# Sliding-window attention and a squared-ReLU MLP: three query loads on ScalarE's DMA queue instead of SyncE's

## The chip, the cores and the metric

The kernel runs on one core of a Trainium2 chip. A core has a matrix engine (TensorE, PE in the profile), a vector engine (VectorE, DVE), an activation engine (ScalarE, ACT), a general engine (GpSimd, POOL) and a sequencer that mainly issues transfers (SyncE, SP). Each takes its own instructions in order. They wait for each other by semaphores. Transfers between memory (HBM) and the core's SBUF go through 16 DMA engines. SP, ACT and POOL can each issue a transfer on a queue of their own; the profile calls SP's queue q1, ACT's q10 and POOL's q0.

The metric is the time of one execution on the device, in microseconds (us). Lower is better.

## The reference

Four batches of eight heads, 768 tokens, head dimension 64. Each query sees the first 4 keys (the sinks) and the last 128 keys up to its own. The heads are then joined to a 3072 x 512 matrix, which goes through two matrix products with a squared ReLU between them.

```python
scores = scale * np.matmul(q, k.transpose(0, 1, 3, 2))
keep = is_sink | in_window            # pos < 4, or 0 <= i - j < 128
scores = np.where(keep, scores, -1e9)
a = softmax(scores)
attn = np.matmul(a, v)
x = attn.transpose(0, 2, 1, 3).reshape(3072, 512)
out = np.maximum(x @ w_in, 0.0) ** 2 @ w_out      # 512 -> 2048 -> 512
```

## The kernel before

The batches are worked through one after another. Attention of batch b + 1 is interleaved with the MLP of batch b, so that PE always has something. Heads go in pairs: pair m is heads 2m and 2m + 1, so there are four pairs, 0 to 3. For each pair, keys and queries must stand transposed in SBUF (the tile qkT), with the head dimension on the partitions.

Only batch 0, and of it the first 512 tokens, concerns the change. Its keys and queries come in eight loads of 256 KB, one for each pair and each of keys and queries, all in float32 (`load_qk`, line 305, the issue on line 315). Four tiles `qr` take them: pairs 0 and 2 share a tile for the keys and one for the queries, pairs 1 and 3 two others. Everything else of the inputs (values, weights, the rest of keys and queries) is loaded by POOL's queue, which converts to bfloat16 on the way.

After a load has landed, one engine converts it to bfloat16 and regroups it (`regroup`, line 404, by the helper `copy` on lines 178 to 183; the profile shows qs<-qr). PE transposes the pair's keys and queries into a PSUM bank pt (line 426). ACT and DVE each copy one half of that bank into qkT (`unload`, line 451; qkT<-pt). Then PE can compute scores of the first 256 tokens (line 538, ps<-qkT; with the mask added as a bias on line 531), ACT takes the exponential (line 559), PE multiplies by the values (line 619).

What runs where and in which order is not found at run time. Every piece of work is an operation with a number, and the string `ORDER` (lines 18 to 57) lists numbers with a letter for the engine: `p` PE, `v` DVE, `a` ACT, `g` POOL, `s` SP. `Plan.run` (line 87) issues them in that order, so each engine's instruction stream is the sequence of its letters. `+10` behind a PE operation puts ten filler matmuls ahead of it (`warm`, line 169, profile line L173), which compute nothing that is used; 36 more stand at the start (line 1209). The eight loads are operations 8 to 15, all on SP: keys 0, queries 0, keys 2, queries 2, keys 1, queries 1, keys 3, queries 3. The helper `dma_op` (line 267) makes the operation of a load; its `follow` says that a load must come after the previous one on the same queue.

Who converts what in batch 0, in each engine's order: DVE takes keys 0 and queries 0 (operations 55, 56), then unloads half of pair 0 (59), then queries 2 (66), later queries 3 (71). ACT takes keys 2 (65), then unloads the other half of pair 0 (58), later keys 3 (70). POOL takes keys 1 and queries 1 (60, 61). The first scores on PE (99) need both halves of pair 0.

SP then loads the four sink values of each head for batches 0, 1 and 2 (`vs_in`, line 361); POOL reads those of batch 0 in line 481.

Of the kernel before, what the change touches and what calls it, by code (L numbers as in the profile page):

```python
# [15 lines left out]
ALU = mybir.AluOpType  # L16

ORDER = """
8s 0v 5g 2v 894p+36 1v 6g 55v 9s 4g 3g 56v 57p 10s 65a 11s 12s 59v 58a 99p+10 19g 20g 101a 21g 22g 23g 13s 14s 66v 79p
81a 67p 69v 80p+11 68a 82a 15s 71v 60g 61g 62p+4 63v 100p 7s 70a 72p+9 74v 64a 87p+2 89a 88p 83p 85p 76v 73v 90a 109p  # L20
24g 25g 26g 27g 103a 86v 84v 91p 93p 77p 94v 95p 92v 97p+13 112a 108p 78a 96a 75g 114p+1 98v 105p+1 110a 152p 104g 17s
28g 29g 30g 102v 31g 32g 33g 106p 113v 111v 115p 107v 116v 34g 35g 36g 37g 158p 159a 117p 118a 119p 164p 120v 161p
162a 163a 153a 155p 156v 38g 39g 173p 122p 125p 165v 157v 127v 174a 160a 123v 126v 124a 170p 171v 139p 140p 141a 16s
# [51 lines left out]
class Plan:  # L75
# [5 lines left out]
    def op(self, kind, engines, run, after=(), takes=(), reads=(), dma=None, follow=(), late=()):  # L81
        o = Op(kind, engines.split(), run, after, takes, reads, dma, follow, late)
        o.group, o.idx = self.group, len(self.ops)
        self.ops.append(o)
        return o
# [21 lines left out]
def kernel(  # L107
# [11 lines left out]
    nc = tc.nc  # L119
# [35 lines left out]
    vs_in = consts.tile([32, B, D + 1], FP32)  # L155
# [10 lines left out]
    def tile_of(slot, name, shape, dtype):  # L166
        return pools[slot.pool][slot.buf].tile(shape, dtype, name=name, tag=slot.pool)
# [97 lines left out]
    chained = {}  # L265

    def dma_op(queue, name, run, takes=()):
        o = op("load " + name[0], queue, run, dma=name[0], takes=takes,
               follow=[chained[queue]] if queue in chained and name[0] != "vs_in" else ())
        ops[name] = o  # L270
        if name[0] != "vs_in":
            chained[queue] = o
        o.name = name
        return o
# [3 lines left out]
    def load_w_in(i):  # L278
        c = slice(512 * i, 512 * i + 512)
        w_in_op[i] = dma_op(  # L280
            "pool", ("w_in", i),
            lambda e: nc.gpsimd.dma_start(out=w_in_sb[:, i],
                                          in_=moe_w_in[:, c].rearrange("(a p) f -> p a f", p=128)))

    def load_w_out(i):
        w_out_op[i] = dma_op(
            "pool", ("w_out", i),
            lambda e: nc.gpsimd.dma_start(
                out=w_out_sb[:, 4 * i:4 * i + 4, :],
                in_=moe_w_out[512 * i:512 * i + 512, :].rearrange("(p f) m -> p f m", p=128)))  # L290

    ops, late = {}, {}
    qr_slot, qs_slot = {}, {}
    qn_t, qn_slot, first_tile = {}, {}, {}
    qr_t, qs_t, ex_t, bank_t = {}, {}, {}, {}
# [9 lines left out]
    def load_qk(m, ti):  # L305

        t0, n = GROUPS[0][0]
        share = (m % 2, ti)
        if share not in qr_slot:
            qr_slot[share] = Slot("qr", 2)  # L310

        def run(e):
            if m < 2:
                qr_t[share] = tile_of(qr_slot[share], "qr", [128, 4, n * D], FP32)
            nc.sync.dma_start(out=qr_t[share][:, 2 * (m // 2):2 * (m // 2) + 2, :],
                              in_=(q, k)[ti][0, 2 * m:2 * m + 2, 0:128 * n, :].rearrange("h (p t) d -> p h (t d)", t=n))
        ops["qk", 0, m, ti, 0] = dma_op("sp", ("qk", 0, m, ti, 0), run, [qr_slot[share]] if m < 2 else [])
        qr_slot[0, m, ti, 0] = qr_slot[share]

    def load_tile(b, ti, t, readers=0):  # L320
# [817 lines left out]
    for m in range(2):  # L1138
        for ti in (1, 0):
            load_qk(m, ti)  # L1140
        for ti in (1, 0):
            load_qk(m + 2, ti)
# [104 lines left out]
```

## Time and profile before

| | us |
|---|---|
| median of 3 runs | 210.09 |
| lowest and highest of the 3 | 209.96, 211.04 |
| the profiled execution | 209.37 |
| its span, first to last instruction | 207.7 |

The profile is one execution of the program, recorded by the hardware. Times in its rows are us from the start of the span, unless marked ns. A row of the timeline has the start, the duration, the engine, the line of the code, the operation, what is written and read, and how many instructions were merged; in brackets stands the idle time of the engine ahead of it and what ended it. PEld is PE's loading of weights, SPq and ACTq are the issuing of transfers by SP and ACT. The share of the DMA engines can exceed 1, since one engine can have several packets in hand at once.

### The profile page before, as it was taken

How to read it: one execution, taken by the hardware profiler on the slowest of the kernel's cores; microseconds unless marked ns; L12 is line 12 of the kernel's file. 1: busy time of each engine (PE TensorE's matmuls, PEld its weight loads, DVE VectorE, ACT ScalarE, POOL GpSimd, SP SyncE). 2: the span in 40 equal slices, each digit the busy share in tenths (PEclk: the TensorE clock that was granted, in tenths of full speed). 3: DMA queues.
4: the chain of work that ended last, by engine and by line, in shares of the span. 5: the costliest groups of instructions: out<-in, count | busy, mean ns of one | idle time of the engine just before them, and what ended most of it. 6: DMA issues, size and time to landing. Idle time of an engine off the chain costs nothing.

```text
span 207.7 us, 5646 instructions
## 1 busy us (share of the span) xinstructions
PE 200.7 (97%) x2373; PEld 168.8 (81%) x2373; DVE 164.9 (79%) x303; ACT 129.9 (63%) x169; POOL 93.4 (45%) x136
## 2 busy tenths in 40 slices
PE   7799999999999999999999999999999999999993
PEld 7459997579657966568798889999889999999982
DVE  6377267487998776668989989999997979899953
ACT  2684288747886553698879185499964168694200
POOL 7999275999925998168020019940240000000000
PEclk9999999999999999999999999999999999999999
DMA  5999999999999999999995146995024305000205
GB/s 147 295 185 206 176 197 213 168 171 173 147 145 83 125 108 150 201 158 134 116 203 153 30 152 41 144 195 32 3 51 129 65 14 200 8 0 0 90 14 202
DMA packets 93865, 26.09 MB, mean 126 GB/s; under 512 B 86800, under 2 KB 91536, under 8 KB 93840
## 3 DMA queue, kind: packets, MB, share of 16 engines
q0 software_dynamic: 69248, 12.59, 82.2%
q1 hardware_dynamic: 24032, 12.69, 30.1%
q10 hardware_dynamic: 560, 0.46, 0.7%
q8 instruction: 18, 0.29, 0.6%
q14 instruction: 7, 0.06, 0.1%
HBM read 27.30 MB, written 6.29 MB: 162 GB/s over the span
## 4 chain that ended last, share of the span: by engine, by line
PE 86%; ACT 5%; DVE 4%; DMA 2%; issue 2%; SPq 0%
PE py L1035 27%; PE pm L836 17%; PE pm L696 16%; PE py L925 7%; PE ps L538 5%; PE po L619 5%; ACT expm L559 2%; DMA qr<-in_k_dram 2%; PE pt L436 2%; DVE sg L993 2%; ACT r L707 1%; PE po L594 1%; PE px L664 1%; PE ya L1035 1%; DVE gT_sb L993 1%
## 5 line engine op out<-in xcount | busy, mean ns | idle before, releaser
L559 ACT ACTIVATE expm<-ps 128x1024 bf16<-128x1024 f32 (+1 forms) x48 | 43.6, 952 | 15.3 <-PE ps L538 15.2
L696 PE MATMUL pm<-xT,w_in_sb 128*128 128x256 bf16 (+1 forms) x320 | 44.9, 294 | 0.1
L199 POOL TENSOR_SCALAR_AFFINE_SELECT expm<-expm 128x512 bf16<-128x512 bf16 x30 | 18.4, 644 | 53.3 <-ACT expm L559 53.2
L696 PEld LDWEIGHTS <-w_in_sb 128*128 128x128 bf16 x320 | 34.2, 114 | 6.5 <-issue 1.0
L1035 PEld LDWEIGHTS <-gT_sb 128*128 128x128 bf16 x336 | 30.6, 98 | 4.4 <-issue 0.9
L707 ACT ACTIVATE r<-pm 128x1024 bf16<-128x1024 f32 x17 | 17.3, 1024 | 14.1 <-PE pm L696 14.1
L1035 PEld LDWEIGHTS <-sg 128*128 128x128 bf16 x240 | 22.6, 98 | 2.5
L836 PE MATMUL pm<-xs,w_in_sb 128*128 128x128 bf16 (+1 forms) x256 | 24.2, 246 | 0.1
L836 PEld LDWEIGHTS <-w_in_sb 128*128 128x128 bf16 x256 | 22.4, 114 | 0.3 <-issue 0.2
L341 POOL DMA_DIRECT2D v<-in_v_dram x24 | 22.0, 938 | 0.0
L1035 PE MATMUL py<-wt,gT_sb 128*128 128x256 bf16 x160 | 20.7, 273 | 0.0
L1035 PE MATMUL py<-wt,sg 128*128 128x256 bf16 x160 | 20.7, 273 | 0.0
L858 ACT ACTIVATE gT_sb<-r 128x1024 bf16<-128x1024 bf16 x19 | 19.2, 1056 | 0.9 <-DVE r L904 0.8
L1035 PE MATMUL py<-w_out_sb,gT_sb 128*128 128x256 bf16 x144 | 18.7, 273 | 0.0
L330 POOL DMA_DIRECT2D qn<-in_k_dram x20 | 18.1, 917 | 1.0 <-DMA qn<-in_q_dram 0.7
L330 POOL DMA_DIRECT2D qn<-in_q_dram x20 | 17.9, 919 | 0.4 <-PE po L619 0.3
L635 DVE TENSOR_TENSOR xn_sb<-po,rc 128x512 bf16<-128x512 f32 (+1 forms) x26 | 16.9, 650 | 0.9
L836 PEld LDWEIGHTS <-qkT 128*128 128x128 bf16 x192 | 16.3, 113 | 0.1
L877 DVE TENSOR_TENSOR t<-t,pm 128x512 f32<-128x512 f32 x24 | 15.6, 682 | 0.9 <-PE pm L836 0.7
L538 PE MATMUL ps<-qkT 64*128 64x128 bf16 (+1 forms) x256 | 14.7, 238 | 1.5 <-ACT qkT L180 1.5
L892 ACT ACTIVATE r<-pm 128x1024 bf16<-128x1024 f32 x12 | 11.9, 1023 | 6.4 <-PE pm L836 5.5
L925 PE MATMUL py<-w_out_sb,gT_sb 128*128 128x512 bf16 x64 | 15.3, 380 | 0.0
(96 smaller groups left out, 326.5 us busy)
## 6 DMA issues: line engine op xcount, KB each, us to landing
out_dram<-osb SPq DMA_DIRECT2D x11, 512.0 KB, 3.5
v<-in_v_dram POOLq DMA_DIRECT2D x24, 128.0 KB, 6.1
qn<-in_k_dram POOLq DMA_DIRECT2D x20, 128.0 KB, 7.6
qn<-in_q_dram POOLq DMA_DIRECT2D x20, 128.0 KB, 5.8
w_in_sb<-in_moe_w_in_dram POOLq DMA_DIRECT2D x4, 512.0 KB, 10.1
w_out_sb<-in_moe_w_out_dram POOLq DMA_DIRECT2D x4, 512.0 KB, 10.5
qr<-in_k_dram SPq DMA_DIRECT2D x4, 256.0 KB, 5.6
qr<-in_q_dram SPq DMA_DIRECT2D x4, 256.0 KB, 5.6
```

The source lines that it names most:

```text
L199: nc.gpsimd.affine_select(out=e_tile, in_=e_tile, compare_op=ALU.is_ge, fill=fill, base=i - 1, pattern=[[0, n], [1 if i else -1, 128]], ch ...
L330: nc.gpsimd.dma_start(out=qn_t[b, ti][:, t, :].rearrange("p (h d) -> p h d", d=D), in_=(q, k)[ti][b, :, 128 * t:128 * t + 128, :].rearrang ...
L341: nc.gpsimd.dma_start(out=v_sb[b % 2][:, t, :, 0:D], in_=v[b, :, 128 * t:128 * t + 128, :].rearrange("h p d -> p h d"))
L538: nc.tensor.matmul(ps[:, h2, o:o + w], lhsT=qkT_sb[r, m, 1, c, :], rhs=qkT_sb[r, m, 0, qb:qb + w // 128, :], start=(i == 0 and not biased) ...
L559: nc.scalar.activation(out=x[:, :, o:512], in_=bank_t["s", b, s, m][:, :, o:512], func=AF.Exp, scale=scale)
L635: touch(("po", b, s, m0), e, nc.vector.tensor_tensor(out=xn_sb[:, 2 * s:2 * s + 2, :].rearrange("p i (j q h d) -> q p j i h d", j=2, q=2, ...
L696: nc.tensor.matmul(pm[:, i, :], lhsT=w_in_sb[:, fb // 4, kb, fb % 4:512:4], rhs=xT[:, c0 // 256:(c0 + cw) // 256, kb, :], start=(kb == 0), ...
L707: nc.scalar.activation(out=o, in_=h, func=AF.Relu)
L836: touch(tag, e, nc.tensor.matmul(y[:, bk, i, :], lhsT=weights(name, f0 + i, a), rhs=rhs[:, a, :], start=fresh and i == 0 and a == 0, stop= ...
L858: nc.scalar.activation(out=d, in_=x, func=AF.Square)
L925: touch((b, u), e, nc.tensor.matmul(pm[:, i, :], lhsT=gT_sb[:, fb, 128 * t:128 * t + 128], rhs=w_out_sb[:, fb, :], start=(fb == 0), stop=( ...
L1035: ins = nc.tensor.matmul(y_, lhsT=x[:, i, :], rhs=r_, start=(first or tail and n == 2) and i == 0, stop=i == HB - 1, skip_group_check=not ...
```

## The change

The queries of pairs 2, 1 and 3 (operations 11, 13 and 15) get the letter `a` instead of `s`: ACT issues them, on its own queue. The queries of pair 0 and all keys stay on SP. In `ORDER` the eight loads now stand together near the front; for SP and ACT only the sequence of their own letters counts.

```diff
-8s 0v 5g 2v 894p+36 1v 6g 55v 9s 4g 3g 56v 57p 10s 65a 11s 12s 59v 58a 99p+10 19g 20g 101a 21g 22g 23g 13s 14s 66v 79p
-81a 67p 69v 80p+11 68a 82a 15s 71v 60g 61g 62p+4 63v 100p 7s 70a 72p+9 74v 64a 87p+2 89a 88p 83p 85p 76v 73v 90a 109p
+8s 0v 5g 2v 894p+36 1v 6g 55v 9s 10s 11a 12s 13a 14s 15a 4g 3g 56v 57p 65a 59v 58a 99p+10 19g 20g 101a 21g 22g 23g 66v
+79p 81a 67p 69v 80p+11 68a 82a 71v 60g 61g 62p+4 63v 100p 7s 70a 72p+9 74v 64a 87p+2 89a 88p 83p 85p 76v 73v 90a 109p
...
     def dma_op(queue, name, run, takes=()):
         o = op("load " + name[0], queue, run, dma=name[0], takes=takes,
-               follow=[chained[queue]] if queue in chained and name[0] != "vs_in" else ())
+               follow=[chained[queue]] if queue == "pool" and queue in chained else ())
...
-            nc.sync.dma_start(out=qr_t[share][:, 2 * (m // 2):2 * (m // 2) + 2, :],
-                              in_=(q, k)[ti][0, 2 * m:2 * m + 2, 0:128 * n, :].rearrange("h (p t) d -> p h (t d)", t=n))
-        ops["qk", 0, m, ti, 0] = dma_op("sp", ("qk", 0, m, ti, 0), run, [qr_slot[share]] if m < 2 else [])
+            (nc.scalar if e == "act" else nc.sync).dma_start(
+                out=qr_t[share][:, 2 * (m // 2):2 * (m // 2) + 2, :],
+                in_=(q, k)[ti][0, 2 * m:2 * m + 2, 0:128 * n, :].rearrange("h (p t) d -> p h (t d)", t=n))
+        ops["qk", 0, m, ti, 0] = dma_op("sp act", ("qk", 0, m, ti, 0), run, [qr_slot[share]] if m < 2 else [])
```

The instruction streams show it at two places. First SP, from the start of the kernel, as it was before (qr_190 and qr_254 are the tiles of pairs 0 and 2, qr_282 and qr_310 those of pairs 1 and 3; k and q tell keys from queries):

```order
L315 DMA qr_190<-in_k_dram 128x2x256
L315 DMA qr_254<-in_q_dram 128x2x256
L315 DMA qr_190<-in_k_dram 128x2x256
L315 DMA qr_254<-in_q_dram 128x2x256
L315 DMA qr_282<-in_k_dram 128x2x256
L315 DMA qr_310<-in_q_dram 128x2x256
L315 DMA qr_282<-in_k_dram 128x2x256
L315 DMA qr_310<-in_q_dram 128x2x256
L361 DMA vs_in_178<-in_v_dram 32x1x64 x3
```

The eight loads stand in one queue, keys 2 third, the sink values behind them. The same place on SP after the change (the keys of pairs 1 and 3 have the tile qr_258; lines behind 315 have moved by one):

```order
L315 DMA qr_190<-in_k_dram 128x2x256
L315 DMA qr_254<-in_q_dram 128x2x256
L315 DMA qr_190<-in_k_dram 128x2x256
L315 DMA qr_258<-in_k_dram 128x2x256 x2
L362 DMA vs_in_178<-in_v_dram 32x1x64 x3
L949 DMA out_0_dram<-osb_960 128x1024
```

Keys 0, queries 0 and keys 2 keep their places; keys 1 and 3 and the sink values move up by one, two and three places. Second, ACT from the start of the kernel, before:

```order
L180 ACT_TABLE_LOAD
L180 ACTIVATE qs_279<-qr_190 128x512
L180 ACTIVATE qkT0_179<-pt_261 128x2x256
L559 ACTIVATE expm_305<-ps_286 128x1024
L559 ACTIVATE expm_322<-ps_315 128x2x384
```

Its first work behind the loading of its function table is the regrouping of keys 2, then half the unloading of pair 0. After the change:

```order
L315 DMA qr_254<-in_q_dram 128x2x256
L315 DMA qr_260<-in_q_dram 128x2x256 x2
L180 ACT_TABLE_LOAD
L180 ACTIVATE qs_286<-qr_190 128x512
L180 ACTIVATE qkT0_179<-pt_269 128x2x256
L560 ACTIVATE expm_309<-ps_290 128x1024
```

The queries of pairs 2, 1 and 3, in that order, stand ahead of the table load; the rest of ACT's stream is unchanged. PE, DVE and POOL execute the same instructions in the same order as before.

## The prediction

> **What bounds the kernel now.** I read the page first, for the engine that is busy and the mix of the chain.
>
> ```profile
> span 207.7 us, 5646 instructions
> PE 200.7 (97%) x2373; PEld 168.8 (81%) x2373; DVE 164.9 (79%) x303; ACT 129.9 (63%) x169; POOL 93.4 (45%) x136
> PE 86%; ACT 5%; DVE 4%; DMA 2%; issue 2%; SPq 0%
> ```
>
> TensorE (PE) is busy for 97% of the span, and the chain of work that ended last lies on it for 86%. DMA has 2% of that chain, some 4 us, so the next view is the table of waits, for PE alone over the whole span.
>
> ```profile
> PE ps L538 <- ACT qkT L180: 1.5, 1, 1.5
> PE warm L1209 <- DVE ones L207: 1.1, 1, 1.1
> PE pk L499 <- ACT expm L559: 0.3, 1, 0.3
> ```
>
> After its start, PE waits once for long: 1.5 us, for the unloading of the first transposes by ScalarE (ACT). The longest of its later waits is 0.3 us. So the place to look at is the first 8 us, and anything that makes the first scores later has no slack to fall into. The chain of waits, cut to the first 30 us, tells what stands ahead of that unloading (start, duration, what):
>
> ```profile
> 1.32 0.46 SPq L315
> ...
> 1.82 4.46 DMA qr<-in_k_dram
> ...
> 6.31 0.63 ACT qs L180
> 6.94 0.49 ACT qkT L180
> ...
> 7.47 0.40 PE ps L538 x6
> ```
>
> The load that is issued at 1.82 us, the third on SP's queue, is the keys of pair 2. It lands at 1.82 + 4.46 = 6.28. ACT then regroups them (its first real instruction), unloads half of pair 0's transposes, and PE starts the scores at 7.47. ACT takes its instructions in order, so the unloading of pair 0, whose transposes are done at 5.3 us (below), stands behind the keys of pair 2. **The landing of the third load sets when PE really begins.**
>
> The landings of the later loads stand in the issue lists of three stretches of 0.1 us, each holding the issues that overlap it (last column: us from issue to landing):
>
> ```profile
> qr<-in_q_dram SPq DMA_DIRECT2D x1, 256.0 KB, 5.1
> qr<-in_k_dram SPq DMA_DIRECT2D x1, 256.0 KB, 5.4
> ...
> qr<-in_q_dram SPq DMA_DIRECT2D x1, 256.0 KB, 5.6
> qr<-in_k_dram SPq DMA_DIRECT2D x1, 256.0 KB, 5.8
> ...
> qr<-in_q_dram SPq DMA_DIRECT2D x1, 256.0 KB, 6.2
> ```
>
> The timeline has the issues themselves, the fourth and the last of the eight:
>
> ```profile
> 2.33 0.47 SPq L315 DMA_DIRECT2D qr<-in_q_dram  x1
> ...
> 4.38 0.47 SPq L315 DMA_DIRECT2D qr<-in_q_dram  x1
> ```
>
> With issues 0.51 us apart (4.38 - 2.33 = 2.05 over four), loads four to eight land at 7.43, 8.24, 8.95, 9.67 and 10.58. They land some 0.7 to 0.9 us apart though issued 0.51 apart, and the delay grows from load to load: the data is slower than the issuing. The table of one-microsecond windows says the same (after the window's length: busy time and count of each engine, then granted clock, share of the 16 DMA engines, GB/s):
>
> ```profile
> 2.00:3.00 1.00, 1.00 (x12) 1.00 (x10) 0.81 (x4) 0.09 (x1) 0.93 (x2) 1.00 0.63 218
> 3.00:4.00 1.00, 1.00 (x13) 1.00 (x11) 0.94 (x4) 0.00 (x0) 0.88 (x5) 1.00 1.03 332
> 4.00:5.00 1.00, 1.00 (x19) 0.90 (x17) 0.81 (x2) 0.00 (x0) 1.00 (x3) 1.00 0.81 170
> 5.00:6.00 1.00, 0.97 (x26) 0.74 (x22) 0.66 (x1) 0.00 (x0) 1.00 (x2) 1.00 0.94 301
> 6.00:7.00 1.00, 0.00 (x0) 0.09 (x1) 0.03 (x1) 0.69 (x2) 1.00 (x2) 1.00 1.10 329
> 7.00:8.00 1.00, 0.53 (x8) 0.28 (x7) 0.43 (x1) 0.52 (x2) 1.00 (x2) 1.00 0.98 324
> ...
> 9.00:10.00 1.00, 1.00 (x16) 0.58 (x13) 0.53 (x1) 1.00 (x2) 1.00 (x3) 1.00 2.05 203
> ```
>
> From 3 us on the DMA engines are busy at about 1.0 with this one queue and move 300 to 330 GB/s, but for a dip to 170 between 4 and 5; the last row, with GpSimd's loads in, is used further down.
>
> Two rows of the timeline complete the start: DVE's casts of pair 0 and PE's transposes of them.
>
> ```profile
> 3.65 1.30 DVE L182 CAST qs<-qr 128x512 bf16<-128x512 f32 x2
> ...
> 4.89 0.42 PE L426 MATMUL pt<-ident,qs 64*128 64x64 bf16 x16
> ```
>
> **The change part by part.** *Issue on SP:* three issues leave it, so keys of pairs 1 and 3 are issued at 2.33 and 2.84 instead of 2.84 and 3.87. The first three (keys 0, queries 0, keys 2) keep place and time: the load that gates PE is issued no earlier. Gain on the path: nothing.
>
> *Issue on ACT:* three issues stand ahead of ACT's table load. The nearest rows for an issue on ACT are the stores at the end, and the table load and ACT's next work are here:
>
> ```profile
> 203.31 0.38 ACTq L1119 DMA_DIRECT2D out_dram<-osb  x1
> ...
> 0.81 1.28 ACT L180 ACT_TABLE_LOAD   x1 [0.81 <-PEq L1228]
> 6.31 0.63 ACT L180 ACTIVATE qs<-qr 128x512 bf16<-128x512 f32 x1 [4.22 <-DMA qr<-in_k_dram]
> ```
>
> Three issues cost between 3 x 0.38 = 1.1 us and, at SP's spacing, 3 x 0.51 = 1.5 us. The table load then runs from about 2.3 to 3.6, and ACT idles until 6.28 anyway. Its 4.22 us of waiting hide it; if the keys landed at once, the 1.5 us would show.
>
> *Data:* the queries of pairs 2, 1 and 3 now start beside keys 0, queries 0 and keys 2 instead of behind them. This is the term that counts. With the bytes shared evenly between the two queues, keys 2 are done when six loads' worth has moved, where before three did. Bounds on its landing:
> - Upper: the sixth slot at the pace of before, 8.95 us (third of the issue rows). That is 8.95 - 6.28 = +2.67.
> - Lower for an even share: the dip is gone. Six loads are 6 x 262 KB = 1573 KB. 218 + 332 = 550 KB have moved by 4.0; the rest at some 335 GB/s takes 3.05 us, to 7.05. From the last byte to the reader I add 0.5 us: queries 0 end the first 524 KB at 3.9, and DVE has cast them by 4.95, with about 0.5 us for the cast. So 7.55, or +1.27.
> - Below that only if the shares are not even: then the SP queue keeps its 6.28, and the term is nothing.
>
> I take 8.6 us, +2.3: nearer to the upper end, which is the same bytes on the same engines, and a dip without a visible cause is not one that I may take away; a little below it, since a second queue may fill idle DMA engines there (share 0.81).
>
> That two queues slow each other has one row: when GpSimd's loads start, the stretches of half a microsecond from 8.0 and from 9.0 have
>
> ```profile
> q1 hardware_dynamic: 192, 0.18, 104.9%
> ...
> q0 software_dynamic: 343, 0.04, 136.6%
> q1 hardware_dynamic: 95, 0.08, 49.0%
> ```
>
> SP's queue (q1) falls from 192 to 95 packets beside GpSimd's (q0), though it was then also near its end, so this supports sharing and does not measure it. The Trainium skill, "DMA: Bandwidth & Descriptors", section "Issuing engines are not separate DMA queues", speaks against the change: loads from SP and ACT run on the same 16 DMA engines and interleave, and a second issuer saves only issue time. By that rule the term is the even share above, and the trace agrees as far as these counts go.
>
> *What waits behind.* Queries 0 land in the fourth slot, up to 7.4 instead of 4.4, so VectorE's (DVE) cast and PE's first transposes move by up to 3 us; ACT's unloading must wait for keys 2 all the same, so this is not added. From there the order is that of before: ACT 0.63 + 0.49, scores 1.19 us after the landing. Queries 2 land early, but DVE casts them behind the unloading of pair 0, and PE then works without a break (7.47 to 12.8), so nothing is won back. Further on stand
>
> ```profile
> 9.25 1.18 POOL L183 CAST qs<-qr 128x512 bf16<-128x512 f32 x2
> ...
> 13.66 1.83 POOL L481 TENSOR_TENSOR vs<-vs_in,head_rows 32x130 bf16<-32x130 f32 x4
> ```
>
> GpSimd's casts need keys 1 and queries 1; keys 1 land seventh, 9.67, so the casts and the weight loads behind them slip 0.4 us, while their readers on PE slip 2.3: hidden. The sink values issued last on SP are read at 13.66, over 3 us after the last landing. With no wait of PE over 0.3 us after 7.47, 2.3 us at the start are 2.3 us at the end.
>
> *Sum:* profiled execution 209.37 = 207.7 span + 1.67 around it; span 207.7 + 2.3 = 210.0, run 211.7. That execution lies 0.72 under the median of 210.09, so on the median the forecast is **212.4**, own range 211.3 (+1.27) to 212.8 (+2.67).
>
> **The rivals.**
> 1. *PE's clock falls as well.* PE's warm-up fillers end at 4.95; if queries 0 come at 7.4, PE does next to nothing until the scores at 9.8.
>
> ```profile
> L1209 PE MATMUL warm<-ones x36: 219/311/311, 1.1 to 4.7; 128*128 128x128 bf16 x36
> ...
> 1.13 3.82 PE L1209 MATMUL warm<-ones 128*128 128x128 bf16 x36 [1.13 <-DVE ones L207]
> ...
> L173 PE MATMUL ps<-ident x23: 219/219/230, 5.2 to 12.0; 128*128 128x128 bf16 x23
> ...
> 8.74 0.79 PE L173 MATMUL ps<-ident 128*128 128x128 bf16 x11
> ```
>
> The fillers take 311 ns at first and the same shape 219 from 4.7 on: the first 3.6 us run slow. If that came again at the scores, 3.6 us of PE would do what takes about 36 x 57 ns = 2.0 us (57 ns apart: 11 fillers in 0.79 us, less 219, over ten), so +1.6 on top: 214.0. For it: the gap. Against: ten fillers and 16 transposes stand in the middle of it, and the 1.5 us gap of before left no slow matmul. The Trainium skill, "TensorE: Matmul & The Clock Gate", section "What's actually happening", has the clock halve after an idle window of about 3.4 us; a broken gap of this size is at its edge, and no run here shows one. Chance 0.08.
>
> 2. *The term is small.* The two queues together carry more than one did, or SP's is served first; keys 2 land at 6.3 to 7.2. For it: the DMA share rises to 2.05 when GpSimd's queue joins, so an engine can have two queues in hand. Against: it moves 203 GB/s then, not more. +0 to +0.9, 210.1 to 211.0. Chance 0.20.
>
> 3. *Faster: the dip was SP's queue running short.* If the 170 GB/s between 4 and 5 us come from the one queue, and the queue of SP is served first, keys 2 (786 KB) end at 4.0 + 236/335 = 4.7, land at 5.2, and PE starts 1.1 us earlier: 209.0. It decides only if ACT's loads take nothing from SP's until 4.7. For it: share 0.81 in the dip. Against: no window above moves more than 332 GB/s, and three more loads are in the way. Chance 0.12.
>
> That the change does not do what it says has no chance of its own: in the instruction order the three loads stand on ACT, first in its stream.
>
> **How the numbers follow.** Forecast 0.60, clock 0.08, small 0.20, faster 0.12. A difference under 0.5%, 1.05 us, cannot be told from no change here: faster 0.12, same 0.20, slower 0.68. The range runs from 209.6, which takes in all of the small case, to 213.6, short of the clock case; about 0.2 is left out.
>
> **What would show it.** In the profile after: ACT's first cast (keys 2) starting between 7.6 and 9.0 instead of 6.31, and the scores 1.2 us behind it; PE's one long wait grown to about 3 us or more, split in two by the first transposes; DVE idle ahead of its second cast, for queries 0; DMA near 330 GB/s in each window, no higher; fillers of 219 ns still. It is wrong if keys 2 land at 6.3 or earlier, if two queues move over 400 GB/s, or if the scores start late and the end does not move.

## The result, and the profile after

| | before | after |
|---|---|---|
| median of 6 runs, us | 210.03 (209.60 to 211.38) | 212.96 (211.79 to 213.14) |
| profiled execution, us | 209.37 | 212.87 |
| its span, us | 207.7 | 211.1 |

The ratio is 1.0111, with a 95% interval of 1.0069 to 1.0153: slower. The two profiled spans are 3.4 us apart. The page of the kernel after shows a mark that the page of before does not have, in the row of granted clocks (tenths of full speed in 40 slices of the span, 5.3 us each):

```profile
span 211.1 us, 5640 instructions
PE 202.8 (96%) x2368; PEld 169.9 (80%) x2373; DVE 165.0 (78%) x303; ACT 130.0 (62%) x169; POOL 92.4 (44%) x136
PEclk9669999999999999999999999999999999999999
PE 85%; ACT 5%; DVE 3%; DMA 3%; issue 2%; SPq 0%
```

The second and third slices have 6: PE's clock was cut there. The chain of waits of the first 20 us, as it was shown of before, now reads (start, duration, what):

```profile
1.82 5.55 DMA qr<-in_k_dram
...
7.40 0.63 ACT qs L180
8.03 0.50 ACT qkT L180
...
8.57 0.61 PE ps L539 x6
9.18 0.76 PE ps L532 x2
...
10.79 1.29 PE ps L173 x11
...
16.30 2.44 ACT expm L560 x3
```

Keys 2 are issued at 1.82 as before and land at 7.38 instead of 6.28; the scores start at 8.57 instead of 7.47. That is +1.10. But the third block of exponentials, 16.30 here, stood at 12.82 before. The rows of before for the same steps:

```profile
7.87 0.43 PE ps L531 x2
...
8.81 0.72 PE ps L173 x11
...
12.82 2.44 ACT expm L559 x3
```

Between the first scores and these exponentials before took 5.35 us, after 7.73. The same eleven fillers took 0.72 and then 1.29 us, two bias matmuls 0.43 and then 0.76. So of 3.48 us lost by then, 1.10 are the later landing and 2.38 a slower PE. The windows of the kernel after give both (columns as in the prediction):

```profile
4.00:5.00 1.00, 0.76 (x19) 0.58 (x17) 0.43 (x1) 0.00 (x0) 1.00 (x4) 1.00 1.10 387
5.00:6.00 1.00, 0.18 (x8) 0.06 (x5) 0.18 (x1) 0.00 (x0) 1.00 (x2) 1.00 1.10 364
...
7.00:8.00 1.00, 0.79 (x10) 0.63 (x11) 0.97 (x2) 0.60 (x2) 1.00 (x3) 0.69 1.09 346
8.00:9.00 1.00, 0.43 (x6) 0.23 (x5) 0.27 (x1) 0.52 (x2) 1.00 (x3) 0.50 1.79 240
...
14.00:15.00 1.00, 1.00 (x25) 0.78 (x19) 0.69 (x1) 1.00 (x3) 0.80 (x3) 0.90 1.92 175
```

The granted clock is half from 7.38 (0.69 of the window from 7) to 14.2 (0.90 of the window from 14). The column does not show the slow start: it reads 1.00 over the first fillers of every kernel here, which take about 311 ns instead of 219. The dip in the DMA rate between 4 and 6 us, 170 and 301 GB/s before, is gone: 387 and 364. That the two queues share the engines is seen directly in the list of queues of the kernel after, from 4.5 to 5.0 us (packets, MB, share of the 16 engines):

```profile
q10 hardware_dynamic: 96, 0.10, 55.2%
q1 hardware_dynamic: 97, 0.09, 53.5%
```

From 3 to 7 us it is 747 packets for SP's queue (q1) and 767 for ACT's (q10). PE's waits are the likely reason why the clock went; experiment 1 tests it:

```profile
PE pt L427 <- DVE qs L182: 1.8, 2, 1.5
...
PE ps L539 <- ACT qkT L180: 0.8, 1, 0.8
```

The one wait of 1.5 us has become 2.6 us of waiting: 1.8 us in two waits for DVE's casts (DVE casts keys 0 at 4.41 instead of 3.65 and queries 0 at 5.82 instead of 4.42) and 0.8 for ACT.

The six executions bear this out. Four have a mean granted clock of 0.984 over the span and took 212.87 to 213.14; two have 0.991 and 0.992 and took 211.79 and 211.92. A mean of 0.984 over 211.1 us is 6.8 us at half speed, 0.992 half as much, and the executions with the shorter cut are 1.2 us faster.

### The profile page after: what moved, and what is told of

Same layout as the page of the kernel before. It is cut to its first block, busy times and chain, and to the rows that moved or that the text cites. A ratio compares the mean times of both kernels' runs of the same rounds, so it can differ in the third digit from the quotient of the medians.

```text
span 211.1 us, 5640 instructions
## 1 busy us (share of the span) xinstructions
PE 202.8 (96%) x2368; PEld 169.9 (80%) x2373; DVE 165.0 (78%) x303; ACT 130.0 (62%) x169; POOL 92.4 (44%) x136
## 4 chain that ended last, share of the span: by engine, by line
PE 85%; ACT 5%; DVE 3%; DMA 3%; issue 2%; SPq 0%
PE py L1036 27%; PE pm L837 17%; PE pm L697 16%; PE py L926 7%; PE ps L539 5%; PE po L620 5%; DMA qr<-in_k_dram 3%; ACT expm L560 2%; PE pt L437 2%; DVE sg L994 2%; ACT r L708 1%; PE po L595 1%; PE px L665 1%; PE ya L1036 1%; PE ps L532 1%
## 5 line engine op out<-in xcount | busy, mean ns | idle before, releaser
L539 PE MATMUL ps<-qkT 64*128 64x128 bf16 (+1 forms) x256 | 15.4, 245 | 0.8 <-ACT qkT L180 0.8
L926 PE MATMUL py<-w_out_sb,gT_sb 128*128 128x512 bf16 x59 | 14.7, 380 | 0.4 <-issue 0.2
```

The costliest lines, as they stand in the source:

```text
L539: nc.tensor.matmul(ps[:, h2, o:o + w], lhsT=qkT_sb[r, m, 1, c, :], rhs=qkT_sb[r, m, 0, qb:qb + w // 128, :], start=(i == 0 and not biased) ...
L926: touch((b, u), e, nc.tensor.matmul(pm[:, i, :], lhsT=gT_sb[:, fb, 128 * t:128 * t + 128], rhs=w_out_sb[:, fb, :], start=(fb == 0), stop=( ...
```

## The experiments

Theory A: the loss has two parts, 1.1 us from keys 2 sharing the DMA engines with loads that are not needed yet, and 2.4 us from PE's clock, which falls because PE idles longer. Theory B: the late loads cost the whole, and the clock falls on time that was lost anyway. Rival C: issuing on ACT, or a second queue, costs in itself. Ratios are against the kernel before on the same chip, with their 95% interval; medians stand beside them.

**1. Keep PE busy.**

```diff
-... 894p+36 ...
+... 894p+60 ...
```

> The changed kernel with 60 instead of 36 filler matmuls at the start, so that PE stays busy until about 6.2 us. Theory A (the loss of the change has two parts: keys 2 land 1.1 us later because the bytes are shared, and PE's clock is halved from 7.4 to 14.2 us, which costs 2.4 us more): the clock stays at 1.0, keys 2 still land near 7.4, the first scores start near 8.6, and the time is before + 1.1, ratio about 1.005 (1.003 to 1.008). Theory B (the late loads alone cost the 3 us and the half clock falls on time that PE would have waited anyway): clock 1.0, time as the changed kernel, ratio 1.011 to 1.014.

Measured: 1.0040 (1.0014 to 1.0067), median 210.73 against 209.86. The chain of waits and the windows of this kernel:

```profile
8.52 0.38 PE ps L539 x6
...
13.85 2.44 ACT expm L560 x3
...
7.00:8.00 1.00, 0.88 (x26) 0.66 (x19) 0.75 (x2) 0.67 (x2) 1.00 (x2) 1.00 1.10 348
```

The clock stays at 1.00, the scores start at 8.52, nearly as late as in the change, and the exponentials stand at 13.85: 1.03 us behind the kernel before instead of 3.48. The loss falls from 2.9 us to 0.9 while the loads are as late as they were. That is A; B is out. (The 60 fillers end at 6.88, and the chain goes by them and by DVE's cast of queries 2, which the scores of pair 0 do not read. By the timeline ACT's half of pair 0 ends at 8.45 and PE starts 0.05 us later, as it does in the kernel before at 7.42 and 7.47; so keys 2, which ACT reads at 7.33, set the start here too, as far as the profile tells.)

**2. Take fillers away from the kernel before.**

```diff
-... 894p+36 ...
+... 894p+12 ...
```

> The kernel before with 12 instead of 36 filler matmuls at the start: the loads are untouched. Theory A: keys 2 land near 6.3 us as before, the clock comes up late, and the time grows by 1 to 3 us by the clock alone, ratio 1.005 to 1.015. Theory B: the loads land as before, so the time is as before within 0.5 us, ratio 0.998 to 1.002.

Measured: 1.0060 (1.0035 to 1.0085), median 211.40 against 209.86. Its chain of waits:

```profile
1.83 4.48 DMA qr<-in_k_dram
...
7.50 0.61 PE ps L538 x6
...
9.72 1.29 PE ps L173 x11
...
14.33 2.44 ACT expm L559 x3
...
10.00:11.00 1.00, 1.00 (x11) 0.95 (x9) 0.78 (x2) 0.64 (x2) 1.00 (x2) 1.00 2.12 169
```

The loads are untouched: keys 2 land at 6.31, the scores start at 7.50. The fillers inside run at the slow pace (1.29 us for eleven), and the exponentials come 1.51 us late. The clock alone, with no load moved, costs 1.5 us at the end. Here it is raised late, not lost, and only the durations of the matmuls show it: the granted clock (third figure from the end of the last row) reads 1.00 while the eleven fillers run slow.

**3. One queue, the same sharing written as an order.**

```diff
-8s 0v ... 55v 9s 10s 11a 12s 13a 14s 15a 4g ...
+8s 0v ... 55v 13s 9s 11s 10s 15s 12s 14s 4g ...
```

> All eight loads on SP's queue, with queries 1 and queries 2 in front of keys 2 (keys 0, queries 0, queries 1, queries 2, keys 2, queries 3, keys 1, keys 3). Theory A (what delays keys 2 is the bytes moved ahead of them, whatever the queue): keys 2 land in the fifth slot, 7.0 to 8.3 us, PE starts the scores 0.7 to 2 us late and its clock may fall; ratio 1.003 to 1.015. Rival C (the loss comes from issuing on ACT or from two queues at once): keys 2 land as late but by no more than 8.3, so no split there; the split is the dip: if it needs a single queue, the GB/s of the window from 4 to 5 us is again under 250 here, as it was before, and over 330 only with two queues.

The order is not quite what the expectation says. Operation 13 is queries 1 and stands ahead of operation 9, queries 0, so the queue carries keys 0, queries 1, queries 0, queries 2, keys 2. Keys 2 are fifth as planned, but queries 0 are third instead of second.

Measured: 1.0144 (1.0106 to 1.0183), median 213.22 against 209.86. The chain of waits, then three windows, then one of PE's waits:

```profile
2.85 5.68 DMA qr<-in_k_dram
...
4.00:5.00 1.00, 0.86 (x19) 0.69 (x16) 0.29 (x1) 0.00 (x0) 1.00 (x4) 1.00 0.92 283
5.00:6.00 1.00, 0.04 (x3) 0.00 (x0) 0.00 (x0) 0.00 (x0) 1.00 (x2) 1.00 0.97 275
6.00:7.00 1.00, 0.11 (x8) 0.12 (x8) 0.59 (x1) 0.00 (x0) 1.00 (x2) 1.00 0.95 211
...
PE pt L427 <- DVE qs L182: 1.9, 1, 1.9
```

With two query loads put ahead of them on the one queue, keys 2 land at 8.53, and the clock is cut again. So bytes ahead of keys 2 delay them without any second queue. The clock says less: DVE casts queries 0 at 6.24 instead of 4.42, PE waits 1.9 us for that, and this is due to the place of queries 0, not of keys 2. Keys 2 land later than expected (8.3 at most), which fits the low rate that is there again: 283, 275 and 211 GB/s from 4 to 7 us, against 387, 364 and 348 with the two queues of the change. For the rate of the DMA engines in this stretch, the second queue was a gain.

**4. Hold ACT's loads back until keys 0 are there.**

```diff
-... 9s 10s 11a 12s 13a 14s 15a 4g ...
+... 9s 10s 895a 11a 12s 13a 14s 15s 4g ...
+    def first_act(e):
+        nc.scalar.activation(out=scratch, in_=qr_t[0, 1][:, 0, 0:1], func=AF.Copy)
```

> The changed kernel, but ACT first loads its table and reads one element per partition of keys 0, and only then issues queries 2 and queries 1; queries 3 are last on SP's queue. So nothing stands beside keys 0 and queries 0, and little beside keys 2. Theory A: keys 0 and queries 0 land as before (3.6 and 4.4), keys 2 at 5.2 to 6.5, the clock stays at 1.0; ratio 0.994 to 1.002. Rival C (issuing on ACT or a second queue costs in itself): ratio over 1.005, or keys 2 after 7 us.

Measured: 1.0119 (1.0082 to 1.0156), median 212.66 against 209.86. I expected 0.994 to 1.002, and this missed. The timeline and two windows:

```profile
3.68 0.96 ACTq L315 DMA_DIRECT2D qr<-in_q_dram  x2
6.71 0.63 ACT L180 ACTIVATE qs<-qr 128x512 bf16<-128x512 f32 x1 [2.83 <-DMA qr<-in_k_dram]
...
9.66 0.43 DVE L182 CAST qs<-qr 128x512 bf16<-128x512 f32 x1 [3.62 <-DMA qr<-in_q_dram]
...
4.00:5.00 1.00, 1.00 (x19) 0.81 (x17) 0.83 (x2) 0.00 (x0) 1.00 (x4) 1.00 0.82 158
...
7.00:8.00 1.00, 0.12 (x4) 0.12 (x5) 0.00 (x0) 0.82 (x2) 1.00 (x2) 0.84 1.03 362
```

While SP's queue is alone, the dip is back (158 GB/s), and keys 2 land at 6.7, later than in the kernel before. The clock is cut from 7.7, while PE waits 1.9 us, to 7.88, for ACT's half of pair 0. Queries 2, issued too late at 3.68, hold DVE until 9.64 and with it PE's next transposes. By its ratio the run goes with rival C; its trace has other causes, keys 2 late by the dip, the clock, and the late queries, and my price for A left them out. It does not decide between A and C.

**5. All keys on SP, all queries on ACT.**

```diff
-... 55v 9s 10s 11a ...
+... 55v 9a 10s 11a ...
```

> The changed kernel with queries 0 on ACT's queue too: all keys on SP, all queries on ACT, so that the two queues carry the loads in the order in which they are needed (keys 0 beside queries 0, keys 2 beside queries 2, and so on). Theory A (bytes are shared evenly between the queues; a single queue has a dip in its rate near 4 to 6 us, two queues together have none): keys 2 are done with the fourth load's worth, land at 5.6 to 6.2 us, the window from 4 to 5 us moves over 340 GB/s, the clock stays at 1.0, ratio 0.994 to 1.000. Rival C (three issues ahead of the table load, or loads on ACT's queue, cost in themselves): keys 2 after 6.5 us, or ratio over 1.003.

Measured: 0.9937 (0.9907 to 0.9967), median 209.28 against 209.91. One row of ACT's timeline, one window, and one of PE's waits:

```profile
5.79 0.63 ACT L180 ACTIVATE qs<-qr 128x512 bf16<-128x512 f32 x1 [1.59 <-DMA qr<-in_k_dram]
...
4.00:5.00 1.00, 1.00 (x11) 0.89 (x9) 0.64 (x2) 0.20 (x1) 1.00 (x3) 1.00 1.09 386
...
PE pt L427 <- POOL qs L183: 0.3, 1, 0.3
```

This has one more load on ACT than the change, and is faster than the kernel before. C is out. What differs from the change is that the two queues now carry what is needed at the same time: keys 2 are done with the fourth load's worth instead of the sixth, and are read at 5.79. All twelve executions lie between 209.18 and 209.44; those of the kernel before beside them scatter from 209.30 to 212.68. Part of the ratio is this scatter: against the 19 of 29 executions of before whose mean clock was 0.997 or more (median 209.81), the gain is 0.5 us. In the profiled pair it is only 0.1 (spans 207.6 and 207.7): the scores start at 6.96 instead of 7.47, but the third block of exponentials at 12.74 instead of 12.82, since PE waits for GpSimd's casts in between.

**6. The same, with the table load between queries 0 and queries 2 on ACT.**

```diff
-... 55v 9a 10s 11a ...
+... 55v 9a 895a 10s 11a ...
```

> As the run with all keys on SP and all queries on ACT, but ACT loads its function table between queries 0 and queries 2 (a one-element activation forces it there), so that queries 2 start about 1.5 us later and keys 2 have the DMA engines more to themselves. Theory A: keys 2 land at 5.0 to 5.7, queries 2 at 6 to 7, ratio 0.992 to 0.999. Rival: the dip comes back as soon as one queue has nothing to move, keys 2 land at 6.0 or later, ratio 0.998 to 1.003.

Operation 895 here reads a constant that DVE sets, and not keys 0. Measured: 0.9953 (0.9928 to 0.9979), median 209.27 against 209.91. Keys 2 are read at 5.69. Nothing was gained over the run before it, and the edit did not do what it was meant to: the timeline has the next two issues on ACT's queue at 1.39, beside the table load (1.33 to 2.61) and not behind it.

**7. The change with the table load first.**

```diff
-... 9s 10s 11a 12s 13a ...
+... 9s 10s 895a 11a 12s 13a ...
```

> The change, but ACT loads its function table first (a one-element activation forces it), so that its three loads are issued from about 2.3 instead of 0.8 us. Theory A: keys 0 and queries 0 land nearly as before (3.6 and 4.4 to 5.0), keys 2 at 5.5 to 6.7, the clock depends on where PE's gap falls; ratio 0.996 to 1.004 with the clock at 1.0, 1.4 to 2.4 us more where it is halved. Rival B (what costs is that the queries of pairs 2, 1 and 3 are on ACT at all): ratio as the change, 1.011.

Measured: 1.0103 (1.0051 to 1.0156), median 212.75 against 209.91. Inconclusive for the same reason:

```profile
0.81 1.28 ACT L1215 ACT_TABLE_LOAD   x1 [0.81 <-PEq L1234]
1.12 0.99 ACTq L315 DMA_DIRECT2D qr<-in_q_dram  x2
...
8.04 0.63 ACT L180 ACTIVATE qs<-qr 128x512 bf16<-128x512 f32 x1 [5.72 <-DMA qr<-in_k_dram]
```

ACT issued two of its loads at 1.12, while the table was loading, only 0.3 us later than the change does. Keys 2 land at 8.02, 0.64 us later than in the change, which nothing here explains, and the clock is cut for 3.4 us instead of 6.8. As a test of later issues it failed; the ratio is that of the change, with another split between the two parts.

**8. Only queries 2 on ACT.**

```diff
-... 11a 12s 13a 14s 15a 4g ...
+... 11a 12s 13s 14s 15s 4g ...
```

> Only queries 2 on ACT's queue, the other seven loads on SP's: one third of the change. Theory A: one load's worth is moved ahead of keys 2 instead of three, so keys 2 are fourth, land at 5.8 to 7.1 us (the lower end without the dip, the upper with it), ratio 0.998 to 1.004. Rival B (any load beside keys 0 and queries 0 costs the whole): keys 2 at 7.3 and the clock halved, ratio 1.008 to 1.014.

Measured: 0.9972 (0.9942 to 1.0001), median 209.62 against 209.91: a third of the change costs nothing that shows, and rival B is out. ACT reads keys 2 at 6.33, the time of before, though one load more has moved by then; the window from 4 to 5 us has 382 GB/s. Its loss in the sharing and its gain from the missing dip cancel. The profiled execution took 210.7, 1.1 over the median, and it is not keys 2 that made it slow:

```profile
1.33 4.22 DMA qr<-in_q_dram
...
6.45 1.18 PE ps L173 x10
...
9.79 1.06 PE ps L173 x11
```

Queries 0 land at 5.55, and PE's fillers run at the slow pace until about 10.5 (ten in 1.18 us; eleven took 0.72 in the kernel before), with a granted clock of 1.00 in all these windows. The scores start 0.16 us later than in the kernel before, the third block of exponentials 1.31 us later. So this is the late clock of experiment 2, with keys 2 in good time.

The queues of this run limit what may be said of the dip. From 4 to 5 us SP's queue moved 344 of the 403 packets, and from 5 to 6 all of them, at 363 GB/s. A queue that is alone need not be slow.

**9. The alternating order, and GpSimd's casts earlier.**

The difference from experiment 5:

```diff
-... 101a 21g 22g 23g 66v ... 71v 60g 61g 62p+4 ...
+... 101a 21g 66v ... 71v 60g 61g 22g 23g 62p+4 ...
```

> All keys on SP, all queries on ACT as before in this study, and GpSimd's casts of pair 1 moved ahead of its loads of two value tiles: PE waited 0.3 us for these casts when the loads alternated. Theory A (the early landing of keys 2, 0.5 us before the old one, was held up there): the casts start at 7.4 to 8.0 instead of 9.0, the wait goes, the time falls by 0.2 to 0.6 us against the alternating order, ratio 0.990 to 0.996. Rival: the value tiles or the MLP weights, issued 1.4 us later, are now waited for; ratio 0.995 to 1.000.

Measured: 0.9942 (0.9919 to 0.9965), median 208.79 (208.66 to 209.04) against 209.72. It has the lowest median, but by the ratios to the kernel before it cannot be told from the alternating order alone (0.9937), which ran on another chip. The profiled spans are 207.0 and 207.6. GpSimd's timeline and PE's longest wait behind the start:

```profile
7.63 1.17 POOL L183 CAST qs<-qr 128x512 bf16<-128x512 f32 x2 [0.39 <-DMA qr<-in_k_dram]
...
PE ps L539 <- DVE qs L182: 0.3, 1, 0.3
```

The casts start at 7.63 instead of 8.97 and now wait for the load itself; PE no longer waits for them, nor for the value tiles issued later, and the third block of exponentials starts at 12.12 instead of 12.74. In the trace, then, what the alternating order gained at the start now arrives.

**10. More fillers in the kernel before.**

```diff
-... 894p+36 ...
+... 894p+44 ...
```

> The kernel before with 44 instead of 36 fillers, loads untouched. If part of its runs are slow because PE's clock is raised late or falls back (theory A: the clock depends on how long PE is busy without a gap), the longer busy stretch makes such runs rarer: the median stays within 0.3 us of 209.9 and the share of runs above 210.9 falls below 1 in 10. If those runs have another cause (rival), their share stays near 3 in 10.

Measured: 0.9981 (0.9952 to 1.0010), median 209.81 against 209.72. The highest of its twelve executions is 210.09. Of the 23 of the kernel before beside them, 17 took 209.35 to 209.93 and six 211.04 to 212.28. The six have a mean granted clock of 0.991 or 0.992, the 17 of 0.997 or more. The tail is gone, as A expects (if the share were still six in 23, twelve executions would miss it with a chance of about 0.03): the kernel before already sits near the edge at which PE's clock is lost.

## Why the prediction was right in its time, and where its sum was off

- *The place.* Right: keys 2, the third load on SP's queue, set the start of the scores, and PE passes the delay on to the end. The landing moved by 1.10 us and the scores by 1.10.
- *The data term.* The mechanism, sharing between the queues, was right (experiments 3, 5 and 8: what counts is how much moves ahead of keys 2). Its size was not. I took 8.6 us for the landing, near the pace of before; it measured 7.38, 0.17 us below the lower end of 7.55. The step that failed is "a dip without a visible cause is not one that I may take away". It went with the second queue, in every run in which two queues moved packets between 4 and 5 us. +2.3 should have been +1.1.
- *The clock.* The first rival, given 0.08 and a price of 1.6 us, happened, and cost 2.38. Its argument, the gap left by late queries 0, was right; the reasons against it, that fillers and transposes break the gap and that the gap of before had no effect, did not carry over. It was also priced for one stretch at half speed; in four of six executions there were two.
- *The sum.* +2.3 stood for 1.1 + 2.4 with the half-speed part counted as nothing. The two errors go opposite ways, and the median, +2.9, came out 0.6 us above the forecast. That it came so near is luck: the place and the sharing were foreseen, the size of either part was not. With the clock kept up (experiment 1) the forecast of the likeliest case would have been 1.4 us too high: the loss is 0.9 us, below what I called a slower kernel.
- *The signs.* Three of those named came out otherwise: ACT's first cast started at 7.40, ahead of the 7.6 to 9.0; the DMA engines moved up to 387 GB/s, not 330; the fillers among the first scores took up to 314 ns, not 219. PE's wait was split as forecast, but is 2.6 us, short of 3.
- *The faster rival.* Half of it was true: the dip came only where SP's queue had been alone from the start. The other half, SP's queue served first, was not. Experiment 5 shows the order in which the first half alone is enough to win.
- *What was hidden.* The three issues on ACT took 0.81 to 2.36, the table load ended at 3.67, and both stayed hidden. GpSimd's casts started at 8.87, not later.

Why a single queue has the dip stays open. It was seen in all five kernels that had one queue at work until then (the kernel before and experiments 2, 3, 4 and 10: 158 to 283 GB/s from 4 to 5 us) and in none of the seven with two (376 to 387), and nothing here shows its cause. That the queue is alone is not enough for it: SP's queue moved 363 GB/s alone from 5 to 6 us in experiment 8, and 329 from 6 to 7 in the kernel before.

## What to carry to other kernels

A second queue does not make room on the DMA engines for loads that are not needed yet: put on it what is needed beside the first queue's loads, not what comes three loads later. Price a wait at the start of a kernel twice, once for its length and once for what PE's clock does after it; two short waits can cost more by the clock than by their length. Where executions of a kernel scatter by half a per cent or more, look at the granted clock, and at the durations of matmuls of one shape, before explaining a small difference: in experiments 2 and 8 the granted clock read 1.00 while the matmuls ran slow.

## What the runs showed of the hardware that was not expected

**PE's clock falls while PE is half busy, and returns slowly.** Three windows of 3.41 us of the kernel after, cut so that the second begins where the clock falls:

```profile
3.97:7.38 3.41, 1.65 (x36) 1.31 (x34) 1.60 (x3) 0.00 (x0) 3.41 (x7) 1.00 1.09 363
7.38:10.79 3.41, 2.63 (x34) 1.39 (x32) 0.89 (x2) 2.52 (x4) 3.41 (x6) 0.50 1.79 223
10.79:14.20 3.41, 3.41 (x41) 2.29 (x43) 1.02 (x2) 1.92 (x4) 3.26 (x6) 0.50 1.70 187
```

PE was busy for 1.65 of 3.41 us, 48%, and the clock was halved; 2.63 us (77%) at half speed did not bring it back, 3.41 us did. Cut the same way, experiments 4, 3 and 7 lost the clock after 1.71, 1.42 and 1.03 us. In the kernel before the windows from 4.55 and from 4.70 both held 1.90 us (56%), and the clock stayed; where its own window began is not recorded. The Trainium skill, "TensorE: Matmul & The Clock Gate", section "What's actually happening", has the clock halve after an idle window of about 3.4 us that runs free of the kernel. The length agrees: half speed lasted 6.8 us here, and 3.4 us in experiment 7. The word "idle" does not: a window half busy was not enough to keep the clock.

**Two queues moved more than one.** From 4 to 5 us they moved 376 to 387 GB/s in the change and in experiments 1 and 5 to 9, against 158 to 283 with one queue. From 2 to 3 us it was the other way round: 126 to 182 in six of these seven (228 in experiment 7), against 218 to 268. So the premise of the prediction that a second issuer saves only issue time did not hold from 4 to 5 us.

**ACT issues loads past a running table load.** In experiment 7 the loads stand behind the table load and a small activation in ACT's stream. The activation waits for a memset on DVE that ends at 1.08; two of the loads were issued from 1.12, with the table load running to 2.09. In experiment 4 the activation waits for keys 0, and there the loads behind it were held until 3.68. So what held them was the wait, not the work ahead of them.
